# Which engine makes the lower parts in the first token block of a fused attention and two-layer gated network

## The chip, the cores and the metric

The kernel runs on one core of one Trainium2 chip. The metric is the device time of one execution in microseconds; lower is better.

## The reference, cut to what matters

Local attention (chunks of 32 queries, a window of 64 keys with 8 memory keys) gives x of 3072 tokens by 512. Two feed-forward layers follow, all in fp32:

```python
x = attention(q, k, v, mem_k, mem_v)            # 3072 x 512
gate = 1 / (1 + np.exp(-(x @ w_gate)))          # 512 -> 1536
x = (gate * (x @ w_val)) @ w_out                # 1536 -> 512
h = x @ w_in                                    # 512 -> 2048
out = (h * (1 / (1 + np.exp(-h)))) @ w_out2     # 2048 -> 512
```

## The kernel before, in words

**Products in three passes.** Every fp32 operand of a product is split in two: an upper part `hi`, which is the value cast to the matmul's type (ScalarE, `nc.scalar.copy`), and a lower part `lo = src - hi` (a subtraction with both inputs in SBUF). A product is then hi·hi + hi·lo + lo·hi, three matmuls of 128x512 each (helpers `split`, lines 77 to 85, `mm3`, lines 87 to 94, and `proj`, line 252). The upper part must be there before the lower part can be made.

**Stages.** The 3072 tokens are six blocks of 512 (`BLOCKS1`). Attention of the first block runs at the start; that of each later block is spread over the block before it. For each block, 12 iterations f do: pg = x·w_gate (12 matmuls), the sigmoid on ScalarE, pv = x·w_val (12 matmuls), the gate `sg = pv * sg` on VectorE (`gated`, L277), its split into g, and 12 matmuls y += g·w_out for the iteration before (`emit_out1`, L90 to L94). After the six blocks the second layer follows (L658 and L771). The order of each engine's queue is the order in which the program is written (`tc.manual_schedule()`).

**Weights of the first layer.** They arrive in a 64-bit layout and are turned into fp32 only once, during the first block, by 36 `Unit` objects: w_gate, w_val and w_out of each f. One unit is one load of 512 KB into a staging buffer `stg` (four of them), `rebias` on ScalarE (L107), `join`, three VectorE instructions of 128x512 (L115, L118, L122) that write the fp32 tile `t` (two buffers), and `part`, which splits t into the tile `u` that the matmuls read; a w_out unit is also written to DRAM (`keep`) for the later blocks. `Feed.step` (lines 145 to 156) is called three times in each iteration f of the first block and handles three units at once, in this order: `part` of unit k-2, `rebias` of unit k, `join` of unit k-1, then the load of a later unit.

```python
def part(self):
    self.u = self.slot(self.name)
    split(self.u[:, 0], self.u[:, 1], self.t, nc.gpsimd)
    if self.keep is not None:
        nc.sync.dma_start(out=self.keep, in_=self.u.bitcast(F32))
```

So in the first block GpSimd makes the lower parts of the 36 weight tiles and, by the table `GL`, those of the 12 gates g; two of the four lower parts of the first x (`split_x` with `NP = 2`) are GpSimd's as well. From the second block on VectorE makes the gates' lower parts itself, by L85.

**The places that matter.** pv of iteration f+1 is written into the PSUM bank that the gate of iteration f read, so TensorE waits there for VectorE's L277. In each iteration VectorE runs two joins before L277 and one behind it; the attention of the next block adds its reductions and products (L202, L203, L210 to L213, L236) in some iterations.

Of the kernel before, what the change touches and what calls it, by code (L numbers as in the profile page):

```python
# [8 lines left out]
F32 = mybir.dt.float32  # L9
# [3 lines left out]
ALU = mybir.AluOpType  # L13
# [16 lines left out]
BLOCKS1 = [512] * 6  # L30
NB2 = 3
NPAIR = NF2 // 2
GL = range(12)
NH = ()
NI = 7
LV = 1
# [11 lines left out]
def moe_kernel(ctx: ExitStack, tc: tile.TileContext, qh, kh, vh, wg, wv, wo, w2i, w2o, out):  # L48
    nc = tc.nc
# [29 lines left out]
    def split(hi, lo, src, lo_eng, hi_eng=nc.scalar):  # L79

        if hi_eng is nc.scalar:
            nc.scalar.copy(hi, src)  # L82
        else:
            hi_eng.tensor_copy(hi, src)
        lo_eng.tensor_tensor(out=lo, in0=src, in1=hi.bitcast(F32), op=ALU.subtract)  # L85
# [11 lines left out]
    class Unit:  # L97
# [26 lines left out]
                op0=ALU.logical_shift_left, op1=ALU.bitwise_or,  # L124
            )

        def part(self):
            self.u = self.slot(self.name)
            split(self.u[:, 0], self.u[:, 1], self.t, nc.gpsimd)
            if self.keep is not None:  # L130
                nc.sync.dma_start(out=self.keep, in_=self.u.bitcast(F32))

    class Feed:
# [10 lines left out]
        def step(self):  # L144
            k, u = self.n, self.units
            if k >= len(u) + 2:
                return
            self.load(k + 1)
            if 0 <= k - 2 < len(u):
                u[k - 2].part()  # L150
            if k < len(u):
                u[k].rebias()
            if 0 <= k - 1 < len(u):
                u[k - 1].join()
            self.load(k + self.AHEAD)
            self.n += 1

# [23 lines left out]
    def att_scores(t, ps_sc, e):  # L181
        sc = ps_sc(f"sc{t}")
        scv = sc.rearrange("p (c2 a k) -> p c2 a k", c2=2, a=4)
        qb, kt = q_t.pop(t), k_t.pop(t)
        for c2 in range(2):
            for a in range(4):
                for cp in range(2):
                    c = 2 * c2 + cp
                    nc.tensor.matmul(  # L189
                        scv[cp * 64 : cp * 64 + 64, c2, a],  # L190
                        qb[:, 4 * a + c].rearrange("p u q -> p (u q)"),
                        kt[:, a, c],
                        start=True,
                        stop=True,
                    )
        if t % TPB == 0:
            nc.vector.memset(scv[0:64, 0, :, NMEM : NMEM + LEFT], NEG)
        if t % TPB == TPB - 1:
            nc.vector.memset(scv[64:128, 1, :, WIN - RIGHT : WIN], NEG)
        s3 = sc.rearrange("p (g k) -> p g k", k=WIN)  # L200
        m = att.tile([P, 8, 1], F32, tag="m", name=f"m{t}", bufs=2)
        nc.vector.tensor_reduce(m, s3, axis=AX.X, op=ALU.max)  # L202
        nc.vector.tensor_tensor(out=e, in0=s3, in1=m.to_broadcast([P, 8, WIN]), op=ALU.subtract)  # L203
        nc.scalar.activation(out=e, in_=e, func=AF.Exp, scale=SCALE)
        e_t[t] = e

    def att_norm(t, eng=nc.vector):
        e = e_t[t]
        r = att.tile([P, 8, 1], F32, tag="r", name=f"r{t}", bufs=2)
        nc.vector.tensor_reduce(r, e, axis=AX.X, op=ALU.add)  # L210
        nc.vector.tensor_scalar_add(r, r, 1e-9)
        nc.vector.reciprocal(r, r)
        eng.tensor_tensor(out=e, in0=e, in1=r.to_broadcast([P, 8, WIN]), op=ALU.mult)  # L213

    def att_turn(t, ps_pt, at):
        e = e_t.pop(t).rearrange("p g k -> p (g k)")
        pt = ps_pt(f"pt{t}")
        for i in range(4):
            nc.tensor.transpose(pt[:, i * P : (i + 1) * P], e[:, i * P : (i + 1) * P], ident)
        nc.scalar.copy(at.rearrange("p a b q -> p (a b q)"), pt)  # L220
        at_t[t] = at

    def att_pv(t, ps_px, xt, off):
        at, vb = at_t.pop(t), v_t.pop(t)
        px = ps_px(f"px{t}")
        for c in range(4):
            for j in range(4):
                q0 = 64 * (c % 2) + 32 * (j % 2)
                nc.tensor.matmul(  # L229
                    px[32 * j : 32 * j + 32, c * P : (c + 1) * P],  # L230
                    at[:, c // 2, j // 2, q0 : q0 + 32],
                    vb[c * len(vb) // 4][:, :, c % (4 // len(vb)), j],
                    start=True,
                    stop=True,
                )
        nc.vector.transpose(  # L236
            out=xt[:, :, off : off + P].rearrange("p k (c q) -> p c k q", c=4),
            in_=px.rearrange("p (c k q) -> p c k q", c=4, k=4),
        )
# [33 lines left out]
        nc.scalar.activation(out=sg[:, :n], in_=psg[:, :n], func=AF.Sigmoid)  # L273
        return sg

    def gated(sg, psv, n, name, pool, bufs, lo_eng=nc.vector):
        nc.vector.tensor_tensor(out=sg[:, :n], in0=psv[:, :n], in1=sg[:, :n], op=ALU.mult)  # L277
        g = pool.tile([P, 2, 512], F32R, tag="g", name=f"g{name}", bufs=bufs)
        split(g[:, 0, :n], g[:, 1, :n], sg[:, :n], lo_eng)
        return g  # L280


    with tc.manual_schedule():
# [3 lines left out]
        p1 = p1_cm.__enter__()  # L287
# [53 lines left out]
        units = []  # L341
# [31 lines left out]
        def idle(n):  # L373
            for _ in range(n):
                nc.tensor.transpose(warm[:, :P], ident, ident)

        def prefetch(t):
            if t < NTILE:
                att_load_qk(t, qA, k_tile(t))

        def prefetch_v(t):
            if t < NTILE:
                att_load_v(t, vA)

        idle(22)
        for i in range(n0 + 2):
            if i < n0:
                att_scores(i, ps_y, es[i])
                idle(NI)
            if 0 <= i - 2 < n0:  # L390
                at = hold[0].tile([P, 512], F32, tag="sg", name=f"at{i - 2}", bufs=3)
                att_turn(i - 2, ps_a, at.rearrange("p (a b q) -> p a b q", a=2, b=2))
                idle(NI if i < 4 else 0)
            if 0 <= i - 1 < n0:
                att_norm(i - 1, nc.gpsimd if i - 1 in NQ else nc.vector)
            if 0 <= i - 3:
                att_pv(i - 3, ps_y, x32[0], (i - 3) * P)
                idle(NI if i < 4 else 0)
            if i == 1:
                prefetch(n0)  # L400
            if i == 4:
                prefetch_v(n0)
            if i == n0:
                units[0].rebias()
                units[0].join()
            if i == n0 + 1:
                units[0].part()
                units[1].rebias()
        att_pv(n0 - 1, ps_y, x32[0], (n0 - 1) * P)
        idle(NJ)  # L410
        x = split_x(x32.pop(0), BLOCKS1[0], "x0", NP, NH)
        units[1].join()
        units[2].rebias()
        feed1.n = 3
        feed1.step()
# [3 lines left out]
        for bi in range(NB1 - 1):  # L419
            n = BLOCKS1[bi + 1] // P  # L420
# [78 lines left out]
        g_t, wo_u, yacc = {}, {}, {}  # L499
# [296 lines left out]
                    done(A22, dp)  # L796


        pending = None
        prep = prepare2()  # L800
        xgen = None
        for bi, n in enumerate(BLOCKS1):
            last = bi == NB1 - 1
            if last:
                att_cm.__exit__(None, None, None)
                xr_cm = tc.tile_pool(name="xr", bufs=1, side="right")
                xr = xr_cm.__enter__()
                xgen = x_parts(0, *load_y0())
            for f in range(NF1):
                it = 3 * (bi * NF1 + f)  # L810

                def steps(i):
                    run_events(it + i)
                    if bi == 0:
                        feed1.step()
                    elif (it + i) % 3 != 0:
                        next(prep, None)
                    if last and (i == 2 and 1 < f < NF1):

                        if f >= 3:  # L820
                            next(xgen, None)

                psg = ps_m(f"pg{bi}_{f}")
                proj(psg, U1["g", f].u, x, n, late=None if bi else (0, 1) if f == 0 else (1, 0))
                sg = sigmoid(psg, n, f"{bi}_{f}")
                steps(0)
                psv = ps_m(f"pv{bi}_{f}")
                proj(psv, U1["v", f].u, x, n, late=None if bi else (1, 0))
                steps(1)
                if f == NF1 - 1 and not last:  # L830
                    x = split_x(x32.pop(bi + 1), BLOCKS1[bi + 1], f"x{bi + 1}")
                g_t[bi, f] = gated(sg, psv, n, f"{bi}_{f}", p1, 2, nc.gpsimd if bi == 0 and f in GL else nc.vector)
                if last and f == NF1 - 1:
                    for _ in range(NRING - 1):
                        next_granule()
                if pending is not None:
                    emit_out1(*pending)
                pending = (bi, f)
                steps(2)

        for _ in prep:
            pass
# [96 lines left out]
```

## Time and profile before

| what | value |
|---|---|
| median of 3 runs (lowest, highest) | 1166.29 us (1165.51, 1167.08) |
| the profiled execution's own time | 1165.85 us |
| its span, first to last instruction | 1164.1 us |
| TensorE matmul busy | 1138.2 us, 98% |
| VectorE busy | 695.6 us, 60%, 965 instructions |
| ScalarE busy | 487.4 us, 42% |
| GpSimd busy | 124.5 us, 11%, 94 instructions |
| first block: first pg to the second block's first pg | 27.70 to 160.54 us of the span |

Engines in the rows: PE is TensorE, DVE is VectorE, ACT is ScalarE, POOL is GpSimd, SP issues the DMAs. The shares are means over the whole span; the first block is about a ninth of it and has another balance than the rest, so it is read by windows of its own.

### The profile page before, as it was taken

The numbers are of one execution on the slowest core, as the hardware profiler recorded it, in microseconds if no ns is written. First come the engines' busy times: TensorE is split into PE (matmuls) and PEld (weight loads), VectorE is DVE, ScalarE is ACT, GpSimd is POOL, SyncE is SP. The second block draws the span as 40 slices with busy tenths as digits, with TensorE's granted clock in tenths as the row PEclk, the third lists the DMA queues.
The fourth block names the chain that finished last, engine by engine and source line by source line (L and its number), as shares of the span: only waits on it lengthen the run. The fifth ranks groups of instructions, "written<-read, shape, count | busy, mean of one in ns | idle before, by whom it ended". The sixth has DMA issues, their size and how long they took to land.

```text
span 1164.1 us, 16020 instructions
## 1 busy us (share of the span) xinstructions
PE 1138.2 (98%) x6319; PEld 927.7 (80%) x6319; DVE 695.6 (60%) x965; ACT 487.4 (42%) x708; POOL 124.5 (11%) x94
## 2 busy tenths in 40 slices
PE   8889999999999999999999999999999999999998
PEld 7667777888888888888887888888888888888887
DVE  7999965455555554554564534347944369634665
ACT  3555544334434433443343224445434454344442
POOL 2545530000000000000000001111001110011000
PEclk9999999999999999999999999999999999999999
DMA  9777767667656666766565356566655575655552
GB/s 314 244 238 246 242 218 238 208 206 227 224 194 212 219 227 194 242 213 203 199 205 211 120 188 199 190 239 237 228 199 192 205 282 215 227 193 203 208 204 86
DMA packets 79210, 248.51 MB, mean 213 GB/s; under 512 B 7584, under 2 KB 23968, under 8 KB 69920
## 3 DMA queue, kind: packets, MB, share of 16 engines
q1 hardware_dynamic: 79136, 247.49, 62.4%
q8 instruction: 50, 0.82, 0.3%
q14 instruction: 24, 0.20, 0.0%
HBM read 199.23 MB, written 48.23 MB: 213 GB/s over the span
## 4 chain that ended last, share of the span: by engine, by line
PE 83%; DVE 12%; DMA 3%; issue 1%; ACT 0%; SPq 0%; DVEq 0%; ACTq 0%
PE o L771 20%; PE c L658 20%; PE pv L263 13%; PE pg L263 13%; PE y L90 5%; PE y L92 5%; PE y L94 5%; PE sc L189 1%; PE px L229 1%; DVE t_wg L122 1%; DVE t_wo L122 1%; DVE t_wv L122 1%; DVE stg_wv L118 1%; DVE stg_wo L118 1%; DVE stg_wg L118 1%; DMA v<-in_vh_dram 1%
## 5 line engine op out<-in xcount | busy, mean ns | idle before, releaser
L658 PE MATMUL c<-xp,wr 128*128 128x512 f32 x1008 | 229.1, 389 | 0.0
L771 PE MATMUL o<-gf,wr 128*128 128x512 f32 x1008 | 229.0, 389 | 0.0
L263 PE MATMUL pv<-x,w 128*128 128x512 f32 x864 | 216.1, 400 | 13.0 <-DVE sg L277 11.4
L658 PEld LDWEIGHTS c<-xp,wr 128*128 128x128 f32 x1008 | 189.2, 188 | 39.3
L771 PEld LDWEIGHTS o<-gf,wr 128*128 128x128 f32 x1008 | 189.2, 188 | 39.3
L263 PE MATMUL pg<-x,w 128*128 128x512 f32 x864 | 210.6, 392 | 1.6 <-POOL x L85 0.9
L263 PEld LDWEIGHTS pv<-x,w 128*128 128x128 f32 x864 | 162.9, 191 | 51.9 <-issue 14.3
L263 PEld LDWEIGHTS pg<-x,w 128*128 128x128 f32 x864 | 160.4, 188 | 38.2 <-ACT x L82 1.5
L85 DVE TENSOR_TENSOR gf<-g,gf 128x1024 fp32r<-128x1024 f32 x84 | 103.8, 1239 | 49.9 <-ACT gf L82 49.6
L82 ACT CAST gf<-g 128x1024 fp32r<-128x1024 f32 x84 | 88.1, 1053 | 86.9 <-PE o L771 73.3
L678 POOL TENSOR_TENSOR s<-s,s 128x512 f32<-128x512 f32 x24 | 35.9, 1497 | 820.7 <-ACT s L677 820.7
L82 ACT CAST g<-sg 128x512 fp32r<-128x512 f32 x72 | 44.7, 621 | 156.8 <-DVE sg L277 156.8
L273 ACT ACTIVATE sg<-pg 128x512 f32<-128x512 f32 x72 | 42.9, 596 | 74.8 <-PE pg L263 61.7
L630 DVE TENSOR_TENSOR s<-c,s 128x512 f32<-128x512 f32 x48 | 33.2, 691 | 65.1 <-PE c L658 63.1
L90 PE MATMUL y<-g,wor 128*128 128x512 f32 x240 | 66.3, 397 | 0.6 <-DVE y L532 0.6
L85 DVE TENSOR_TENSOR g<-sg,g 128x512 fp32r<-128x512 f32 x60 | 41.5, 692 | 41.7 <-ACT g L82 41.7
L92 PE MATMUL y<-g,wor 128*128 128x512 f32 x240 | 64.3, 390 | 0.0
L94 PE MATMUL y<-g,wor 128*128 128x512 f32 x240 | 64.2, 389 | 0.0
L277 DVE TENSOR_TENSOR sg<-pv,sg 128x512 f32<-128x512 f32 x72 | 49.3, 684 | 21.3 <-PE pv L263 21.2
L633 DVE TENSOR_TENSOR g<-g,g 128x1024 f32<-128x1024 f32 x48 | 58.4, 1216 | 0.0
L636 ACT ACTIVATE g<-s 128x512 f32<-128x512 f32 x48 | 30.3, 632 | 54.1 <-DVE s L630 54.1
L92 PEld LDWEIGHTS y<-g,wor 128*128 128x128 f32 x240 | 45.1, 188 | 9.6
(120 smaller groups left out, 1127.3 us busy)
## 6 DMA issues: line engine op xcount, KB each, us to landing
wr<-w2o_d SPq DMA_DIRECT2D x42, 1024.0 KB, 4.8
wor<-wo_d SPq DMA_DIRECT2D x60, 512.0 KB, 4.7
wr<-w2i_d SPq DMA_DIRECT2D x24, 1024.0 KB, 5.0
wr<-w2i_d SPq DMA_DIRECT2D x24, 768.0 KB, 4.4
w2o_d<-coo SPq DMA_DIRECT2D x56, 256.0 KB, 2.8
w2i_d<-coi SPq DMA_DIRECT2D x24, 512.0 KB, 3.0
qA<-in_qh_dram SPq DMA_DIRECT2D x21, 512.0 KB, 4.9
k<-in_kh_dram SPq DMA_DIRECT2D x21, 512.0 KB, 5.5
```

Source lines behind the costliest of these rows:

```text
L82: nc.scalar.copy(hi, src)
L85: lo_eng.tensor_tensor(out=lo, in0=src, in1=hi.bitcast(F32), op=ALU.subtract)
L90: nc.tensor.matmul(o, w_hi, x_hi, start=first, stop=False)
L92: nc.tensor.matmul(o, w_hi, x_lo, start=False, stop=False)
L94: nc.tensor.matmul(o, w_lo, x_hi, start=False, stop=last)
L263: nc.tensor.matmul(o[:, :n], w[:, pw, kt * P : (kt + 1) * P], x[kt][:, px, :n], start=i == 0, stop=i == len(steps) - 1,)
L273: nc.scalar.activation(out=sg[:, :n], in_=psg[:, :n], func=AF.Sigmoid)
L277: nc.vector.tensor_tensor(out=sg[:, :n], in0=psv[:, :n], in1=sg[:, :n], op=ALU.mult)
L633: nc.vector.tensor_tensor(out=o, in0=a, in1=b_, op=ALU.subtract)
L658: nc.tensor.matmul(o, w[:, pw, i % 4, kt * P : (kt + 1) * P], X[i][:, px, kt], start=first and j == 0, stop=j == 5, skip_group_check=not f ...
L678: nc.gpsimd.tensor_tensor(out=s5, in0=s5, in1=s1, op=ALU.add)
L771: nc.tensor.matmul(c[at[i], dp], w[:, pw, pl, dp * P : (dp + 1) * P], f[:, px, pl], start=i in (A11, S1, S2) and pp == 0 and j == 0, stop= ...
```

## The change

GpSimd's 48 lower parts (36 weight tiles, 12 gates) go to VectorE. `part` is cut in two: `high` makes the upper part on ScalarE where `part` stood, and `rest` makes the lower part on VectorE, behind the join of the next unit; the DMA that keeps a w_out tile follows it. A gate's lower part is put in a list in the first block, and made after the third `Feed.step` of the iteration. The two lower parts of the first x stay on GpSimd.

```diff
-GL = range(12)
...
-        def part(self):
+        def high(self):
             self.u = self.slot(self.name)
-            split(self.u[:, 0], self.u[:, 1], self.t, nc.gpsimd)
+            nc.scalar.copy(self.u[:, 0], self.t)
+
+        def rest(self):
+            nc.vector.tensor_tensor(
+                out=self.u[:, 1], in0=self.t, in1=self.u[:, 0].bitcast(F32), op=ALU.subtract
+            )
             if self.keep is not None:
                 nc.sync.dma_start(out=self.keep, in_=self.u.bitcast(F32))
...
             self.load(k + 1)
+
             if 0 <= k - 2 < len(u):
-                u[k - 2].part()
+                u[k - 2].high()
             if k < len(u):
                 u[k].rebias()
             if 0 <= k - 1 < len(u):
                 u[k - 1].join()
+            if 0 <= k - 2 < len(u):
+                u[k - 2].rest()
             self.load(k + self.AHEAD)
...
-    def gated(sg, psv, n, name, pool, bufs, lo_eng=nc.vector):
+    def gated(sg, psv, n, name, pool, bufs, rest=None):
+
         nc.vector.tensor_tensor(out=sg[:, :n], in0=psv[:, :n], in1=sg[:, :n], op=ALU.mult)
         g = pool.tile([P, 2, 512], F32R, tag="g", name=f"g{name}", bufs=bufs)
-        split(g[:, 0, :n], g[:, 1, :n], sg[:, :n], lo_eng)
+        nc.scalar.copy(g[:, 0, :n], sg[:, :n])
+
+        def lo():
+            nc.vector.tensor_tensor(
+                out=g[:, 1, :n], in0=sg[:, :n], in1=g[:, 0, :n].bitcast(F32), op=ALU.subtract
+            )
+
+        lo() if rest is None else rest.append(lo)
         return g
...
             if i == n0 + 1:
-                units[0].part()
+                units[0].high()
                 units[1].rebias()
...
         units[1].join()
+        units[0].rest()
         units[2].rebias()
...
-        pending = None
+        pending, rests = None, []
...
-                g_t[bi, f] = gated(sg, psv, n, f"{bi}_{f}", p1, 2, nc.gpsimd if bi == 0 and f in GL else nc.vector)
+                g_t[bi, f] = gated(sg, psv, n, f"{bi}_{f}", p1, 2, None if bi else rests)
...
                 steps(2)
+                while rests:
+                    rests.pop()()
```

VectorE's queue at the start of the first block, before (x_0 and x_1 are the first tokens, t_wg_384 and t_wv_455 the fp32 tiles of the first gate and value weights, stg their staging buffers):

```order
L85 TENSOR_TENSOR x_0_443<-x_0_113,x_0_443 128x512
L85 TENSOR_TENSOR x_1_446<-x_0_113,x_1_446 128x512
L115 TENSOR_SCALAR stg_wv_138<-stg_wv_138 128x512
L118 SCALAR_TENSOR_TENSOR stg_wv_138<-stg_wv_138 128x512
L122 SCALAR_TENSOR_TENSOR t_wv_455<-stg_wv_138 128x512
L115 TENSOR_SCALAR stg_wg_140<-stg_wg_140 128x512
L118 SCALAR_TENSOR_TENSOR stg_wg_140<-stg_wg_140 128x512
L122 SCALAR_TENSOR_TENSOR t_wg_463<-stg_wg_140 128x512
```

and the same place now (the tile numbers and lines are shifted; L131 is `rest`, w_413 the weight tile that the first pg and pv read):

```order
L84 TENSOR_TENSOR x_0_442<-x_0_113,x_0_442 128x512
L84 TENSOR_TENSOR x_1_445<-x_0_113,x_1_445 128x512
L114 TENSOR_SCALAR stg_wv_138<-stg_wv_138 128x512
L117 SCALAR_TENSOR_TENSOR stg_wv_138<-stg_wv_138 128x512
L121 SCALAR_TENSOR_TENSOR t_wv_454<-stg_wv_138 128x512
L131 TENSOR_TENSOR w_413<-t_wg_384,w_413 128x512
L114 TENSOR_SCALAR stg_wg_140<-stg_wg_140 128x512
L117 SCALAR_TENSOR_TENSOR stg_wg_140<-stg_wg_140 128x512
L121 SCALAR_TENSOR_TENSOR t_wg_462<-stg_wg_140 128x512
L131 TENSOR_TENSOR w_413<-t_wv_454,w_413 128x512
L114 TENSOR_SCALAR stg_wv_142<-stg_wv_142 128x512
```

The first gate weight's lower part, which the first pg reads from its second matmul on, now stands behind the join of the first value weight.

VectorE's queue of one iteration without attention (f = 5), before:

```order
L277 TENSOR_TENSOR sg_4_858<-pv_4_870,sg_4_858 128x512
L115 TENSOR_SCALAR stg_wg_790<-stg_wg_790 128x512
L118 SCALAR_TENSOR_TENSOR stg_wg_790<-stg_wg_790 128x512
L122 SCALAR_TENSOR_TENSOR t_wg_918<-stg_wg_790 128x512
L115 TENSOR_SCALAR stg_wv_843<-stg_wv_843 128x512
L118 SCALAR_TENSOR_TENSOR stg_wv_843<-stg_wv_843 128x512
L122 SCALAR_TENSOR_TENSOR t_wv_950<-stg_wv_843 128x512
L115 TENSOR_SCALAR stg_wo_868<-stg_wo_868 128x512
L118 SCALAR_TENSOR_TENSOR stg_wo_868<-stg_wo_868 128x512
L122 SCALAR_TENSOR_TENSOR t_wo_972<-stg_wo_868 128x512
L277 TENSOR_TENSOR sg_5_937<-pv_5_956,sg_5_937 128x512
```

and its beginning now (L285 is the gate, L290 the gate's lower part):

```order
L285 TENSOR_TENSOR sg_4_858<-pv_4_870,sg_4_858 128x512
L114 TENSOR_SCALAR stg_wg_790<-stg_wg_790 128x512
L117 SCALAR_TENSOR_TENSOR stg_wg_790<-stg_wg_790 128x512
L121 SCALAR_TENSOR_TENSOR t_wg_915<-stg_wg_790 128x512
L131 TENSOR_TENSOR wo_912<-t_wo_890,wo_912 128x512
L290 TENSOR_TENSOR g_4_898<-sg_4_858,g_4_898 128x512
L114 TENSOR_SCALAR stg_wv_842<-stg_wv_842 128x512
L117 SCALAR_TENSOR_TENSOR stg_wv_842<-stg_wv_842 128x512
L121 SCALAR_TENSOR_TENSOR t_wv_949<-stg_wv_842 128x512
L131 TENSOR_TENSOR w_946<-t_wg_915,w_946 128x512
```

Four instructions were added between two gates: one `rest` behind each of the three joins, and the lower part of g behind the first of them. ScalarE's queue has the same 709 rows in the same order in both kernels, and SP's DMAs stand in the same order.

## Rows read from the trace of the kernel before

**Rows 1.** The page: busy us of each engine, share, instructions.

```profile
PE 1138.2 (98%) x6319; PEld 927.7 (80%) x6319; DVE 695.6 (60%) x965; ACT 487.4 (42%) x708; POOL 124.5 (11%) x94
```

**Rows 2.** Windows: length; busy PE, PEld, DVE, ACT, POOL; clock, DMA, GB/s.

```profile
41.90:154.90 113.00, 98.76 (x602) 76.09 (x600) 105.99 (x130) 60.92 (x96) 60.83 (x40) 0.97 0.69 233
163.10:276.10 113.00, 112.66 (x715) 90.91 (x714) 61.45 (x112) 45.09 (x69) 1.29 (x1) 1.00 0.68 231
```

**Rows 3.** Waits, 41.9 to 154.9 us: us in total, times, longest us.

```profile
PE pv L263 <- DVE sg L277: 9.7, 7, 2.2
```

**Rows 4.** Timeline of DVE in the first block: start us, us, engine line op.

```profile
58.58 0.69 DVE L118 SCALAR_TENSOR_TENSOR stg_wv<-stg_wv 128x512 int32<-128x512 int32 x1
59.38 1.60 DVE L122 SCALAR_TENSOR_TENSOR t_wv<-stg_wv 128x512 int32<-128x512 int32 x1
```

**Rows 5.** Timeline of POOL in the first block.

```profile
58.87 1.56 POOL L85 TENSOR_TENSOR w<-t_wg,w 128x512 fp32r<-128x512 f32 x1 [2.62 <-ACT w L82]
```

**Rows 6.** Windows of L122 alone, first and second block: DVE busy, clock, DMA.

```profile
41.90:154.90 113.00, 36.46 (x30) 0.97 0.69 233
180.00:300.00 120.00, 4.84 (x7) 1.00 0.68 224
```

**Rows 7.** Windows of L118 alone, first and second block: DVE busy, clock, DMA.

```profile
41.90:154.90 113.00, 28.12 (x30) 0.97 0.69 233
180.00:300.00 120.00, 4.86 (x7) 1.00 0.68 224
```

**Rows 8.** Windows of L115 alone, first and second block: DVE busy, clock, DMA.

```profile
41.90:154.90 113.00, 20.45 (x31) 0.97 0.69 233
180.00:300.00 120.00, 2.91 (x7) 1.00 0.68 224
```

**Rows 9.** Windows of L213 alone, first and second block: DVE busy, clock, DMA.

```profile
41.90:154.90 113.00, 6.03 (x4) 0.97 0.69 233
180.00:300.00 120.00, 3.46 (x5) 1.00 0.68 224
```

**Rows 10.** Windows of L277 alone, first block.

```profile
41.90:154.90 113.00, 6.80 (x10) 0.97 0.69 233
```

**Rows 11.** Timeline of DVE in the second block.

```profile
171.64 0.69 DVE L85 TENSOR_TENSOR g<-sg,g 128x512 fp32r<-128x512 f32 x1 [0.74 <-ACT g L82]
172.25 0.68 DVE L532 COPY y<-y 128x512 f32<-128x512 f32 x1
176.47 0.69 DVE L118 SCALAR_TENSOR_TENSOR stg_w2i<-stg_w2i 128x512 int32<-128x512 int32 x1
177.19 0.69 DVE L122 SCALAR_TENSOR_TENSOR fi<-stg_w2i 128x512 int32<-128x512 int32 x1
```

**Rows 12.** Timeline of PE, start and end of the first block.

```profile
27.70 2.98 PE L263 MATMUL pg<-x,w 128*128 128x512 f32 x11 [0.62 <-ACT x L82]
33.52 4.61 PE L263 MATMUL pv<-x,w 128*128 128x512 f32 x12 [1.43 <-ACT w L82]
152.26 1.08 PE L229 MATMUL px<-vA,at 128*32 128x128 f32 x32
157.82 1.07 PE L90 MATMUL y<-g,wo 128*128 128x512 f32 x4
160.54 2.99 PE L263 MATMUL pg<-x,w 128*128 128x512 f32 x12
```

**Rows 13.** Timeline of DVE: first join, and gates of iterations 0 and 10.

```profile
32.12 0.69 DVE L122 SCALAR_TENSOR_TENSOR t_wv<-stg_wv 128x512 int32<-128x512 int32 x1
41.22 0.68 DVE L277 TENSOR_TENSOR sg<-pv,sg 128x512 f32<-128x512 f32 x1
154.19 0.68 DVE L277 TENSOR_TENSOR sg<-pv,sg 128x512 f32<-128x512 f32 x1
```

**Rows 14.** Timeline of ACT behind the gate of iteration 2.

```profile
64.48 0.62 ACT L82 CAST g<-sg 128x512 fp32r<-128x512 f32 x1 [2.23 <-DVE sg L277]
65.01 0.62 ACT L82 CAST wo<-t_wo 128x512 fp32r<-128x512 f32 x1
```

## The prediction

> **What bounds the kernel now.** I read the page first: TensorE is busy for 98% of the span and VectorE for 60% [rows 1]. That is a mean, so the next view is the windows. In 113 us of the first block TensorE shows 98.8 us of work and VectorE 106.0 us; in 113 us of the second block TensorE shows 112.7 us and VectorE 61.5 us [rows 2]. The first block is VectorE's, the rest TensorE's. The waits say the same: in the first block TensorE stands 9.7 us in seven waits for L277, the gate, before it may start the next pv [rows 3]. So what VectorE saves between gates in this block, the block saves, down to TensorE's own work there. That work, at the rate of the second block (715 recorded matmuls in 112.7 us), is 602 / 715 x 112.7 = 94.9 us for 113.0 us elapsed.
>
> Next, what fills VectorE. In its timeline the same 128x512 instruction comes in two lengths: L118 at 58.58 us takes 0.69 us, L122 right behind it 1.60 us [rows 4]. GpSimd had started a lower part at 58.87 us [rows 5]. Line by line, against the second block, where GpSimd makes none: L122 takes 36.46 us for 30, against 4.84 us for 7 [rows 6]; L118 28.12 against 4.86 [rows 7]; L115 20.45 for 31, against 2.91 for 7 [rows 8]; L213 6.03 for 4, against 3.46 for 5 [rows 9]. L277, which reads one input from PSUM, stays at 0.68 us for each of 10 [rows 10]. GpSimd's work stretches VectorE's.
>
> **The change, part by part.** I take the stretch from the end of gate 0 (41.90 us) to the end of gate 10 (154.87 us), 112.97 us, then its two ends.
>
> *Removed: the stretching.* The excess over the second block's durations: L122 36.46 - 30 x 0.691 = 15.7; L118 28.12 - 30 x 0.694 = 7.3; L115 20.45 - 31 x 0.416 = 7.6; L213 6.03 - 4 x 0.692 = 3.3 [rows 6 to 9]. Together 33.8 us, beside 40 GpSimd instructions [rows 2], so 0.85 us each. Their own 60.8 us lie beside VectorE and count only through this.
>
> *Removed: a wait for GpSimd's semaphore.* L122 now waits for GpSimd to have read the buffer that it overwrites. It starts 0.80 us behind L118 in the first block [rows 4] and 0.72 us in the second, where there is no such wait [rows 11]. 30 x 0.08 = 2.4 us.
>
> *Added: 40 lower parts on VectorE.* In the second block the same instruction (L85) is 0.69 us long and the next starts 0.61 us behind it [rows 11]. 40 x 0.61 = 24.4 us, all on the path. The upper bound, 0.69 each, is 27.6.
>
> *Sum of the stretch:* -33.8 - 2.4 + 24.4 = -11.8 us, so 101.2 us, still above TensorE's 94.9. As a cross-check, three joins of 1.85 us (L115 0.42 [rows 8] and a gap of 0.10, then 0.72 and 0.61), four lower parts and a gate make 8.6 us for an iteration without attention. TensorE's loop there is pv (2.7 to 2.9), then y (2.72), which must wait until VectorE has made a join and two lower parts (3.1 us behind the gate), then pg (2.7 to 2.9): about 8.7 us. The two are nearly level, so I expect a few tenths of wait on either side, and a new wait of y for the gate's lower part.
>
> *The start.* The first pg reads the weight's lower part from its second matmul on. Before, GpSimd had it ready when pg began at 27.70 [rows 12]. Now it comes behind the join of the first value weight, whose last instruction starts at 32.12 [rows 13]; that join is still stretched, since GpSimd keeps two lower parts of x. It is ready at 32.12 + 0.61 + 0.69 = 33.4, and eleven matmuls follow. Warm, eleven took 2.98 us; the twelve at 33.52, behind a gap of 1.43 us, took 4.61 [rows 12]. Behind a gap of over 5 us I take the slow figure, about 4.3. Then the sigmoid and the next upper part (1.4 us), a lower part, a join, a lower part and the gate: gate 0 ends near 42.95 against 41.90 [rows 13], **+1.05**. With TensorE warm VectorE would set the pace and gate 0 end at about 41.5, -0.4.
>
> *The end.* Before, from gate 10 (end 154.87) to the second block's pg (160.54) it took 5.67 us. Now y(10) waits for its gate's lower part, 3.1 us behind the gate, and takes 2.72 (157.82 to 160.54, [rows 12]): 5.8. TensorE will also come late to that pv, since the last attention product (1.08 us, [rows 12]) then stands ahead of it with no slack left: up to +1.1. I take **+0.9**, bounds +0.1 and +1.2.
>
> *At nothing:* ScalarE does the same work in the same order. The upper part that a lower part waits for is made while VectorE joins: behind the gate ScalarE casts g and then the w_out tile, the two starting 0.53 us apart and each lasting 0.62 [rows 14], 1.2 us against a join's 1.85. The w_out store moves behind `rest` on SP's queue; loads queue behind it, as they do behind GpSimd's instruction now, and have three steps, some 8 us, to land. If one took longer, VectorE's next join would be late.
>
> *Sum:* -11.8 + 1.05 + 0.9 = -9.85. From the profiled execution's 1165.85 us that is **1156.0 us**. The median of the runs before is 0.4 us above that execution, so a median after it may read 0.4 more. The stages behind are TensorE's and shift as they are.
>
> **The rivals.**
>
> *TensorE becomes the bound (0.09).* pv took 4.61 us behind an idle gap instead of some 2.9 [rows 12]; the granted clock is 0.97 of full in the first block's window and 1.00 in the second's [rows 2], so part of the block already runs at 1.2 GHz instead of 2.4. With gaps of about 1 us left in each iteration, half of the ten pv's might be slow: 1.7 us each less the 0.6 to 0.7 us that TensorE has spare, 5 us in all. Time: 1161. Against it: the gaps get shorter than the present ones, up to 2.2 us [rows 3].
>
> *ScalarE's upper part comes late (0.05), slower.* Now VectorE itself waits for the upper part; before, only GpSimd did, and VectorE ran on. Everything behind `rest` on VectorE's queue, the gate too, would stand. Each of 30 `rest` may lose 0.39 us on average before the 11.8 us are gone; at 0.6 us each (ScalarE one cast further behind, [rows 14]) the stretch loses 18 and the time is 1165.85 - 9.85 + 18 = 1174. For it: ScalarE's order puts a gate's cast, which waits for VectorE, ahead of a weight's. Against it: the 1.2 against 1.85 us above.
>
> *VectorE was simply full (0.03), slower.* If the long forms are not GpSimd's doing but belong to this stage (the staging buffers are also written by DMA), 24.4 us come on top and nothing goes: 1165.85 + 24.4 + 2 = 1192. The Trainium skill bears on it: "Perfetto Trace Analysis", section "Optimizing Scalar/DVE Operations", says that work may be taken off a saturated VectorE, even to GpSimd, and adds that the two share a read port, so that this might not help. The first half of that speaks against this change. The rows speak for the second: L277 with its PSUM input is untouched and L213, which reads no staging buffer, is stretched [rows 9, 10].
>
> *No change (0.03):* gains and new stalls of some 10 us cancel, 1165.
>
> **How the numbers follow.** The forecast has 0.80, the partial gain 0.09, no change 0.03, the two slower cases 0.08. About 0.2%, 2.3 us, is what a measurement of this kernel can tell from none. Faster: 0.80 + 0.09 = 0.89; within: 0.03; slower: 0.08. The range's lower end takes the start at -0.4, the end at +0.1 and TensorE's waits at none: 1165.85 - 11.8 - 0.3 = 1153.8, less 0.7, the difference if the cross-check's steps are summed instead of the excesses: 1153. The upper end takes in the rival of TensorE, 1161, and 0.4 for the median: 1161.5. That leaves out some 0.15.
>
> **What would show it.** Right: GpSimd at 46 instructions and VectorE at 1013; L115, L118 and L122 back near 0.42, 0.69 and 0.69 us everywhere but in the first join; the stretch from gate 0 to gate 10 near 101 us; gate 0 about 1 us later, with a gap of over 5 us in the first pg; a new wait of y for the gate's lower part of a few us in sum; nothing changed behind the first block. Wrong: VectorE idle in front of `rest` for ScalarE (the second rival); slow matmuls in many iterations (the first); long forms left (the third); joins waiting for loads.

## The result, and the profile after

Four runs of the changed kernel have a median of 1155.3 us (1154.98 to 1156.31), four of the kernel before 1165.9 us (1165.5 to 1167.08): a ratio of 0.9905, 95% interval [0.9894, 0.9917]. The profiled executions are 10.9 us apart in span, 1164.1 and 1153.2 us.

The page of the changed kernel, the line that answers to [rows 1]:

```profile
PE 1133.1 (98%) x6319; PEld 926.5 (80%) x6319; DVE 685.9 (59%) x1013; ACT 487.8 (42%) x708; POOL 52.1 (5%) x46
```

VectorE has 48 instructions more and is busy 9.7 us less; GpSimd has 48 fewer. Where that happened is in the windows, the stretch from the end of gate 0 (44.15 us) to the end of gate 10 (144.94 us), and 113 us of the second block (columns as in [rows 2]):

```profile
44.15:144.94 100.79, 94.53 (x610) 74.52 (x609) 95.87 (x171) 60.43 (x96) 0.00 (x0) 1.00 0.77 261
152.30:265.30 113.00, 113.00 (x719) 91.83 (x718) 62.22 (x114) 45.27 (x69) 0.00 (x0) 1.00 0.68 229
```

The stretch took 112.97 us before and takes 100.79 us now. VectorE made 41 instructions more in it (the 40 lower parts, and a gate at the window's edge), in 10.1 us less of busy time. The windows of single lines show why, in this order L121, L117, L114 and L220, which were L122, L118, L115 and L213 [rows 6 to 9]:

```profile
44.15:144.94 100.79, 20.78 (x30) 1.00 0.77 261
```

```profile
44.15:144.94 100.79, 20.83 (x30) 1.00 0.77 261
```

```profile
44.15:144.94 100.79, 12.59 (x31) 1.00 0.77 261
```

```profile
44.15:144.94 100.79, 2.77 (x4) 1.00 0.77 261
```

36.46 became 20.78, 28.12 became 20.83, 20.45 became 12.59 and 6.03 became 2.77: 34.1 us of stretching are gone, against 33.8 in the prediction's ledger. The timeline of VectorE in this stretch shows one join with the lower part behind it, and the gate's:

```profile
64.88 0.69 DVE L117 SCALAR_TENSOR_TENSOR stg_wg<-stg_wg 128x512 int32<-128x512 int32 x1
65.61 0.69 DVE L121 SCALAR_TENSOR_TENSOR t_wg<-stg_wg 128x512 int32<-128x512 int32 x1
66.22 0.69 DVE L131 TENSOR_TENSOR wo<-t_wo,wo 128x512 fp32r<-128x512 f32 x1
66.82 0.68 DVE L290 TENSOR_TENSOR g<-sg,g 128x512 fp32r<-128x512 f32 x1
```

L121 starts 0.73 us behind L117 (0.80 before, [rows 4]), and each lower part takes 0.60 or 0.61 us of the queue. The waits in the same stretch:

```profile
PE pv L270 <- DVE sg L285: 5.2, 4, 2.1
PE y L91 <- DVE g L290: 1.0, 3, 0.4
```

TensorE's wait for the gate fell from 9.7 us in seven [rows 3] to 5.2 us in four, and the new wait of y for the gate's lower part is there, with 1.0 us. No wait of VectorE for ScalarE shows in the stretch.

The two ends. TensorE at the start of the first block and at its end (these answer to [rows 12]):

```profile
27.46 0.50 PE L270 MATMUL pg<-x,w 128*128 128x512 f32 x1 [0.51 <-ACT x L81]
33.20 4.67 PE L270 MATMUL pg<-x,w 128*128 128x512 f32 x11 [5.24 <-DVE w L131]
...
145.22 3.01 PE L270 MATMUL pv<-x,w 128*128 128x512 f32 x12
...
150.79 2.88 PE L270 MATMUL pg<-x,w 128*128 128x512 f32 x12
```

The first pg does one matmul and then stands 5.24 us for the weight's lower part. VectorE and ScalarE behind it, first the two lower parts around the wait and gate 0, then ScalarE's sigmoid:

```profile
40.39 0.69 DVE L131 TENSOR_TENSOR w<-t_wg,w 128x512 fp32r<-128x512 f32 x1 [2.91 <-ACT w L128]
...
43.47 0.68 DVE L285 TENSOR_TENSOR sg<-pv,sg 128x512 f32<-128x512 f32 x1
```

```profile
37.96 1.28 ACT L280 ACT_TABLE_LOAD   x1 [4.17 <-PE pg L270]
39.25 0.60 ACT L280 ACTIVATE sg<-pg 128x512 f32<-128x512 f32 x1
39.74 0.61 ACT L128 CAST w<-t_wg 128x512 fp32r<-128x512 f32 x1
```

Gate 0 ends 16.69 us behind the first pg, where it was 14.20 us. At the other end the second block's pg starts 5.85 us behind the end of gate 10, before 5.67.

### The profile page after: what moved, and what is told of

Same layout as the page of the kernel before. It is cut to its first block, busy times and chain, and to the rows that moved or that the text cites. A ratio compares the mean times of both kernels' runs of the same rounds, so it can differ in the third digit from the quotient of the medians.

```text
span 1153.2 us, 15956 instructions
## 1 busy us (share of the span) xinstructions
PE 1133.1 (98%) x6319; PEld 926.5 (80%) x6319; DVE 685.9 (59%) x1013; ACT 487.8 (42%) x708; POOL 52.1 (5%) x46
## 4 chain that ended last, share of the span: by engine, by line
PE 86%; DVE 9%; DMA 3%; issue 1%; ACT 1%; SPq 0%; DVEq 0%; ACTq 0%
PE o L787 20%; PE c L674 20%; PE pg L270 14%; PE pv L270 14%; PE y L89 5%; PE y L91 5%; PE y L93 5%; PE sc L196 2%; PE px L236 1%; DVE w L131 1%; DMA v<-in_vh_dram 1%; DVE stg_wv L117 1%; DVE sg L285 1%; PE pt L226 1%; DVE stg_wo L117 1%
## 5 line engine op out<-in xcount | busy, mean ns | idle before, releaser
L270 PE MATMUL pv<-x,w 128*128 128x512 f32 x864 | 211.2, 393 | 5.2 <-DVE sg L285 5.2
L270 PEld LDWEIGHTS pv<-x,w 128*128 128x128 f32 x864 | 160.0, 188 | 41.9 <-issue 8.6
L290 DVE TENSOR_TENSOR g<-sg,g 128x512 fp32r<-128x512 f32 x72 | 49.8, 691 | 42.6 <-ACT g L287 42.6
L285 DVE TENSOR_TENSOR sg<-pv,sg 128x512 f32<-128x512 f32 x72 | 49.4, 686 | 20.6 <-PE pv L270 20.5
```

The lines of the kernel that those rows point to most:

```text
L270: nc.tensor.matmul(o[:, :n], w[:, pw, kt * P : (kt + 1) * P], x[kt][:, px, :n], start=i == 0, stop=i == len(steps) - 1,)
L290: nc.vector.tensor_tensor(out=g[:, 1, :n], in0=sg[:, :n], in1=g[:, 0, :n].bitcast(F32), op=ALU.subtract)
```

## The experiments

Each is the changed kernel with one edit. "The stretch" is always from the end of gate 0 to the end of gate 10, 100.79 us in the changed kernel; gate 0 is given by its end. Theory: in the first block VectorE's queue sets the pace, and what GpSimd does there lengthens that queue by more than the same work costs on VectorE. Rival: VectorE was simply full, the long forms belong to the stage. Second rival: ScalarE's upper part, or TensorE, sets the pace.

### GpSimd makes the weights' lower parts once more

```diff
             nc.vector.tensor_tensor(
                 out=self.u[:, 1], in0=self.t, in1=self.u[:, 0].bitcast(F32), op=ALU.subtract
             )
+            nc.gpsimd.tensor_tensor(
+                out=self.u[:, 1], in0=self.t, in1=self.u[:, 0].bitcast(F32), op=ALU.subtract
+            )
```

> The changed kernel, in which GpSimd makes each of the 36 weights' lower parts a second time, right behind VectorE's, into the same place with the same values. Nothing is taken from VectorE. Theory (GpSimd's instructions stretch VectorE's by 0.85 us each, and VectorE's join waits 0.08 us more for GpSimd's semaphore): 30 x 0.93 = 28 us in the stretch from gate 0 to gate 10 and 1 or 2 us at the start: about 1184 us, the means of L114, L117, L121 and of the lower parts well above 0.42, 0.69, 0.69, 0.69. Rival (the long forms belong to the stage, not to GpSimd): only the semaphore's 2.4 us, about 1158 us, all forms short.

Measured: 1183.06 us (one run), the stretch 122.54 us, 21.75 us more; gate 0 at 47.42 us. VectorE executes the same instructions as in the changed kernel. Its timeline, with GpSimd's instruction between:

```profile
63.37 0.69 DVE L293 TENSOR_TENSOR g<-sg,g 128x512 fp32r<-128x512 f32 x1
...
63.53 1.68 POOL L134 TENSOR_TENSOR wo<-t_wo,wo 128x512 fp32r<-128x512 f32 x1 [3.62 <-DVE wo L131]
...
63.97 1.53 DVE L114 TENSOR_SCALAR stg_wv<-stg_wv 128x512 int32<-128x512 int32 x1
...
71.03 0.68 DVE L288 TENSOR_TENSOR sg<-pv,sg 128x512 f32<-128x512 f32 x1
...
71.19 1.28 POOL L134 TENSOR_TENSOR w<-t_wv,w 128x512 fp32r<-128x512 f32 x1 [2.03 <-DVE w L131]
...
71.63 1.12 DVE L114 TENSOR_SCALAR stg_wg<-stg_wg 128x512 int32<-128x512 int32 x1
```

The long forms are back, on the instruction that starts while GpSimd's runs: L114 takes 1.53 us there and ends 0.29 us behind GpSimd's end. The one that VectorE has under way when GpSimd starts keeps its length, L293 with its two SBUF inputs too. The timeline of the kernel before shows the same: inside 38 of the 40 GpSimd instructions of the stretch a long form starts; the 29 of L122, L118 and L213 end 0.54 to 0.56 us behind GpSimd's end (60.98 against 60.43 us in [rows 4, 5]), the nine of L115 0.28 to 0.30 us behind it. So VectorE is held until GpSimd is done, and the price is what is left of GpSimd's instruction by then. VectorE's busy time in the stretch rises from 95.87 to 115.17 us, 0.64 us for each of 30, and the semaphore adds the rest. The rival that VectorE was simply full gives 1158 us and falls. The size was overstated: 0.64 rather than 0.85 us. Here GpSimd starts each time right behind VectorE's lower part; in one of three places the gate is under way by then, which is not lengthened, and the L114 behind it meets less of GpSimd's instruction: 1.12 us instead of 1.53.

### VectorE makes the weights' lower parts once more

```diff
             nc.vector.tensor_tensor(
                 out=self.u[:, 1], in0=self.t, in1=self.u[:, 0].bitcast(F32), op=ALU.subtract
             )
+            nc.vector.tensor_tensor(
+                out=self.u[:, 1], in0=self.t, in1=self.u[:, 0].bitcast(F32), op=ALU.subtract
+            )
```

> The changed kernel, in which VectorE makes each of the 36 weights' lower parts twice, the same instruction once more. Theory (VectorE's queue sets the stretch, 0.61 us for each further lower part): 30 x 0.61 = 18.3 us between gate 0 and gate 10 and some 1.8 us at the start: about 1175.4 us. Beside the repeat by GpSimd this gives the price of the same work on either engine: 0.61 against 0.93. Rival (TensorE nearly sets the pace by now, so VectorE has spare time): clearly less than 18 us, under 1168 us.

Measured: 1180.25 us (one run), the stretch 122.53 us, 21.74 more; gate 0 at 46.62 us. The theory's sign and place hold, TensorE hides none of it. The size is 0.72 us each, not 0.61: the repeat writes what the instruction ahead of it wrote, so it starts only behind that one's end.

```profile
62.27 0.68 DVE L131 TENSOR_TENSOR wo<-t_wo,wo 128x512 fp32r<-128x512 f32 x1
62.99 0.69 DVE L134 TENSOR_TENSOR wo<-t_wo,wo 128x512 fp32r<-128x512 f32 x1
63.59 0.69 DVE L293 TENSOR_TENSOR g<-sg,g 128x512 fp32r<-128x512 f32 x1
```

The second starts 0.72 us behind the first, the next, independent one 0.60 behind that. So the two repeats cost the stretch the same 21.7 us, and I may not set 0.61 against 0.93 as the expectation did. What the pair does show is that an instruction which VectorE does not execute costs its queue as much as a dependent one that it does.

### The gates' lower parts on GpSimd again

```diff
-    def gated(sg, psv, n, name, pool, bufs, rest=None):
+    def gated(sg, psv, n, name, pool, bufs, rest=None, lo_eng=nc.vector):
...
         def lo():
-            nc.vector.tensor_tensor(
+            lo_eng.tensor_tensor(
...
-                g_t[bi, f] = gated(sg, psv, n, f"{bi}_{f}", p1, 2, None if bi else rests)
+                g_t[bi, f] = gated(sg, psv, n, f"{bi}_{f}", p1, 2, None, nc.vector if bi else nc.gpsimd)
```

> The changed kernel, with the 12 gates' lower parts of the first block back on GpSimd and the 36 weights' still on VectorE. Theory (a lower part costs VectorE 0.61 us when it makes it and 0.85 us when GpSimd makes it beside): 10 of them lie between gate 0 and gate 10, so the stretch grows by 10 x 0.24 = 2.4 us, from 100.8 to 103.2, and the time is 1157.7 us; some ten or more of VectorE's instructions show the long form again. Rival (VectorE was simply full and its long forms are not GpSimd's doing): VectorE loses 10 x 0.61 us of work and the time falls to 1149 us, no long forms.

Measured: 1159.02 us (1158.81 to 1159.78), ratio to the kernel before 0.9939 [0.9925, 0.9954]. The stretch takes 103.63 us, 2.84 more (expected 2.4). This undoes a quarter of the change, and VectorE, relieved of ten instructions, is the slower for it. In the windows of L121 alone the ten GpSimd instructions show:

```profile
45.12:148.75 103.63, 26.64 (x30) 1.00 0.75 254
```

5.86 us more than the 20.78 of the changed kernel. With L117 (21.73, 0.90 more), L114 (12.96, 0.37 more) and L220 (4.45, 1.68 more) that is 8.8 us for ten, 0.88 each, against 0.60 that VectorE saves: 2.8 us net. The long ones are ten, one for each of GpSimd's: six of L121, two of L220, one each of L117 and L114. The rival's 1149 us is far off. The median is 3.7 us above the changed kernel's, 2.4 were expected: in the profiled executions, 4.8 us apart, 1.0 us more lies ahead of the end of gate 0 and 1.2 us behind the second block's first pg.

### GpSimd only writes

```diff
             nc.vector.tensor_tensor(
                 out=self.u[:, 1], in0=self.t, in1=self.u[:, 0].bitcast(F32), op=ALU.subtract
             )
+            nc.gpsimd.memset(self.t, 0.0)
```

> The changed kernel, in which GpSimd clears each fp32 weight tile t (128x512) when both parts have been made from it, 36 instructions that write SBUF and read nothing; the tile is dead by then. The join that writes the tile next waits for GpSimd's semaphore. Theory A (any GpSimd instruction in SBUF stretches VectorE's): some 0.3 us or more for each of the 30 in the stretch, beside the semaphore's 0.08: 10 to 25 us more, 1165 to 1180 us. Theory B (only GpSimd's reading collides with VectorE's second input): the semaphore's 30 x 0.08 = 2.4 us alone, about 1157.7 us, with L117, L121 and the lower parts at 0.69 us; L114, which has one input and is the fast form, may be touched. The Trainium skill, page "SBUF - State Buffer", section "Who interferes with whom", says that a VectorE instruction with two SBUF inputs collides with a GpSimd instruction that reads SBUF and not with one that only writes it, which is theory B.

Measured: 1160.04 us (one run), the stretch 103.23 us, 2.44 more. That is the 30 x 0.08 us of the semaphore. Few of VectorE's instructions meet the clearing in a way that tells: L291, the gate's lower part, is under way when it starts, and would keep its length beside a subtraction too; L121 never overlaps it. The seven that tell are the L117 behind the clearing of a gate weight's tile:

```profile
62.91 0.42 DVE L114 TENSOR_SCALAR stg_wo<-stg_wo 128x512 int32<-128x512 int32 x1
63.11 0.69 POOL L134 MEMSET t_wg<- 128x512 f32 x1 [2.61 <-DVE w L131]
63.43 0.69 DVE L117 SCALAR_TENSOR_TENSOR stg_wo<-stg_wo 128x512 int32<-128x512 int32 x1
64.23 0.69 DVE L121 SCALAR_TENSOR_TENSOR t_wo<-stg_wo 128x512 int32<-128x512 int32 x1
```

and the same place where GpSimd subtracts, from the run in which it repeats the lower parts:

```profile
67.78 1.39 POOL L134 TENSOR_TENSOR w<-t_wg,w 128x512 fp32r<-128x512 f32 x1 [2.57 <-DVE w L131]
68.14 1.57 DVE L117 SCALAR_TENSOR_TENSOR stg_wo<-stg_wo 128x512 int32<-128x512 int32 x1
```

Held to the clearing's end as it was to the subtraction's, L117 would take some 0.9 us, an estimate from the 0.37 us that are left of the clearing and the 0.55 us behind its end; it takes 0.69 or 0.70 in all seven. L121 starts 0.80 us behind L117 here, where the changed kernel has 0.73: this is the semaphore alone, with nothing stretched. So theory B holds in these seven, for an instruction with two SBUF inputs, as the Trainium skill's page "SBUF — State Buffer" ("Who interferes with whom") has it. The clearing is also shorter than the subtraction (0.5 to 0.7 us against 1.3 to 1.7), so that GpSimd's reading is what makes the difference is argued from one run, and only for a short write. Nothing shows for L114: where it starts beside a clearing, at most 0.14 us of that is left. In these seven places the clearing takes 0.68 to 0.70 us, in the others 0.52 or 0.53: there GpSimd is the one that loses time, whether to L114 or to L117 the run does not tell. The remaining 2.3 us of the run's 4.7 lie outside the stretch; gate 0 alone is 1.3 us later.

### The lower part asked for at once

```diff
             if 0 <= k - 2 < len(u):
                 u[k - 2].high()
+                u[k - 2].rest()
             if k < len(u):
                 u[k].rebias()
             if 0 <= k - 1 < len(u):
                 u[k - 1].join()
-            if 0 <= k - 2 < len(u):
-                u[k - 2].rest()
```

> The changed kernel, with the lower part asked of VectorE right behind the order to ScalarE for the upper part, ahead of the next unit's join instead of behind it. The instructions are the same ones. Theory (the place behind the join is what hides ScalarE): in each iteration VectorE waits about 0.2, 0.75 and 1.2 us at its three weight parts (join to upper part, the last of them behind the gate's cast too), 2.1 us, so 10 iterations cost 21 us: about 1176 us, with a wait of VectorE's lower parts for ScalarE of some 20 us in sum. Rival (TensorE's own work or the loads set the pace, VectorE has slack): under 4 us more, below 1160 us.

Measured: 1176.84 us (one run), the stretch 119.85 us, 19.1 more (expected 21). The waits of VectorE between 46 and 167 us, a window around the stretch (46.62 to 166.47):

```profile
DVE wo L131 <- ACT wo L128: 9.8, 8, 1.7
DVE w L131 <- ACT w L128: 8.4, 10, 1.2
```

18.2 us in 18 waits, with the same instructions: this is the second rival's mechanism, and the place behind the join is what keeps it out of the changed kernel. Moved without that, the work would have cost more than it brought: 1176.84 us is slower than the kernel before.

### The first lower part earlier

```diff
-        x = split_x(x32.pop(0), BLOCKS1[0], "x0", NP, NH)
-        units[1].join()
         units[0].rest()
+        x = split_x(x32.pop(0), BLOCKS1[0], "x0", NP, NH)
+        units[1].join()
```

> The changed kernel, with the first gate weight's lower part made by VectorE ahead of the split of the first x instead of behind the join of the first value weight. Theory (the start's loss is this one instruction's place): the gap of 5.24 us in the first pg goes, gate 0 ends near 40.5 us of the span instead of 44.15, the stretch from gate 0 to gate 10 keeps its 100.8 us, and the time is 1155.3 - 3.6 = 1151.7 us. Rival (the start is set by the loads and the attention in front): the time stays at 1155.3 us, and gate 0 moves by less than 0.5 us.

Measured: 1152.26 us (1151.73 to 1152.67), ratio to the kernel before 0.988 [0.9863, 0.9896]. Gate 0 ends at 40.70 us, 3.45 earlier, and the stretch keeps 101.24 us. VectorE's timeline before the first pg and TensorE's:

```profile
26.76 0.65 DVE L131 TENSOR_TENSOR w<-t_wg,w 128x512 fp32r<-128x512 f32 x1
27.57 1.29 DVE L84 TENSOR_TENSOR x<-x,x 128x512 fp32r<-128x512 f32 x2 [0.16 <-ACT x L81]
28.78 1.52 DVE L114 TENSOR_SCALAR stg_wv<-stg_wv 128x512 int32<-128x512 int32 x1
```

```profile
27.59 2.99 PE L270 MATMUL pg<-x,w 128*128 128x512 f32 x11 [0.50 <-ACT x L81]
```

The lower part fits where VectorE was idle for the upper parts of x, and the gap of 5.24 us is gone. Since the difference to the changed kernel is small, both were measured once more, side by side:

> The changed kernel once more, on the same chip and in the same call as the kernel with the first gate weight's lower part moved forward, so that the two can be set side by side. Expected: 1155.3 us, as before.

> The changed kernel with the first gate weight's lower part ahead of the split of the first x, beside the changed kernel itself. Theory: 3 us under it, 1152.3 us, with intervals that do not touch. Rival (the 3 us between the first runs of the two were the chip's): within 1 us of it.

The changed kernel: 1156.31 us (1154.58 to 1157.12), ratio 0.9912 [0.9897, 0.9926]. With the first lower part earlier: 1152.65 us (1151.85 to 1152.87), ratio 0.9883 [0.9866, 0.9899]. The intervals overlap at their ends, so the expectation that they don't is missed; the runs themselves do not overlap, and the medians are 3.7 us apart, 3.0 in the first pair.

### No GpSimd in the first block at all

```diff
-NP = 2
+NP = 0
```

on top of the edit before.

> The changed kernel with the first gate weight's lower part ahead of the split of the first x, and with all four lower parts of that x on VectorE, so that GpSimd does nothing in the first block. Theory: the first join, which took 1.50, 1.64 and 0.69 us beside GpSimd's two, falls by 2.0 us, and two more lower parts cost VectorE 1.2 us; gate 0 ends 0.8 us before that of the kernel with the first part alone, 1150.9 us. Rival (TensorE's first pg and pv, not VectorE, set gate 0 by then): no difference to the kernel with the first part alone, within 0.3 us.

Measured: 1152.31 us (1150.36 to 1152.82), ratio 0.9877 [0.9859, 0.9895]. The same as with the first part alone; the rival's number holds. The first join is short again (L114 0.42, L117 0.69 us), but gate 0 ends 12.91 us behind the first pg instead of 13.11. Not TensorE holds it, as the rival had it: VectorE waits for the next load, which it did not reach so early before.

```profile
37.73 0.43 DVE L114 TENSOR_SCALAR stg_wo<-stg_wo 128x512 int32<-128x512 int32 x1 [0.31 <-DMA stg_wo<-in_wo_dram]
38.50 0.69 DVE L117 SCALAR_TENSOR_TENSOR stg_wo<-stg_wo 128x512 int32<-128x512 int32 x1 [0.34 <-ACT stg_wo L106]
```

These two waits take 0.65 of the 0.8 us that the edit was worth.

## Why the prediction was right, and which terms were off

The forecast was 1156.0 us, the median 1155.3. The steps one by one, in the profiled executions:

- **What bounds the block.** VectorE from gate to gate: shown by VectorE's repeat, which adds its full price to the stretch, and by the stretch, 100.79 us against 95.87 us of VectorE's busy time and the gaps between its instructions, with TensorE at 94.53.
- **The stretch.** Forecast -11.8 us (-12.5 by the cross-check), measured -12.18. The removed stretching was 34.1 (forecast 33.8); the semaphore 0.07 to 0.08 us each, shown alone by the run in which GpSimd only writes; the added parts 0.60 to 0.61 us.
- **The start: the term that was too small.** Forecast +1.05, measured +2.49 (gate 0 against the first pg; +2.04 in the changed kernel's second trace). The late lower part, the gap and the slow matmuls behind it came as written, with 4.67 us for eleven instead of about 4.3. What was left out is the load of the sigmoid's table on ScalarE: it stands behind the same wait for pg, so its 1.28 us came on top of the sigmoid before the next upper part could be made, and VectorE stood 2.91 us. Before, the load stood in that place too (34.09 us), but VectorE did not wait for ScalarE there. Moving that one lower part takes the loss away, and a little more.
- **The end: too large.** Forecast +0.9, measured +0.18. TensorE was not late at the pv that waits for gate 10: it starts 0.28 us behind the gate's end.
- **Behind the block: forecast nothing, measured -1.15 us**, so the sign "nothing changed behind the first block" failed (span -10.9, of which -9.75 at the second block's first pg: -0.24 before the first pg, +2.49, -12.18 and +0.18). A hint is in SP's queue. There the last w_out store waited for GpSimd's lower part, and the first load of the second layer's weights, issued 1.15 us behind that pg before, is now issued 0.57 us ahead of it. VectorE's wait for it falls from 5.10 to 2.60 us, and TensorE's wait of 0.22 us for VectorE, in front of the transposes of the second block's third iteration, is gone. VectorE's first join and those transposes, before and now:

```profile
168.16 0.43 DVE L115 TENSOR_SCALAR stg_w2i<-stg_w2i 128x512 int32<-128x512 int32 x1 [5.10 <-DMA stg_w2i<-in_w2i_dram]
184.56 0.63 PE L219 MATMUL pt<-ident,e 128*128 128x128 f32 x4 [0.22 <-DVE e L213]
```

```profile
156.45 0.43 DVE L114 TENSOR_SCALAR stg_w2i<-stg_w2i 128x512 int32<-128x512 int32 x1 [2.60 <-DMA stg_w2i<-in_w2i_dram]
173.86 0.60 PE L226 MATMUL pt<-ident,e 128*128 128x128 f32 x4
```

From that pg to these transposes it took 24.02 us before and takes 23.07 now, in the changed kernel's second trace too: 0.95 of the 1.15 us. With the gates' lower parts back on GpSimd the load is issued 0.57 us behind the pg again, VectorE waits 5.56 us for it and the transposes come after 23.78 us. There the w_out store waits for VectorE and not for GpSimd, so it is the late load that goes with the loss, whatever made it late. This was read off the traces and not tried by itself. The other 0.2 us is no more than two executions of the changed kernel differ: the second trace has -0.77 instead of -1.15 behind the block.
- **The rivals.** ScalarE late: possible, and seen, with the lower part asked for at once; kept out by the order. TensorE slow: the granted clock in the stretch is 1.00 (0.97 before); with the same work and more idle time, in the run with the parts asked for at once, it was 0.91. A lower clock need not cost time here: in VectorE's repeat it was 0.93, and the stretch grew by just VectorE's 30 x 0.72 us. VectorE simply full, and with it the rule to unload a full VectorE: refuted from both sides, by GpSimd's repeat and by the gates' return to GpSimd.

The errors are +1.4 us at the start, -0.7 at the end, -0.4 in the stretch, -1.15 behind the block and -0.24 ahead of the first pg; together they make -1.05. The stretch, which is the mechanism, was right; that the total is closer than the start alone is luck.

## What to carry to other kernels

A helper engine is free only if it doesn't lengthen the instructions of the engine that it relieves: compare the same instruction's duration in a stage with the helper and in one without, multiply, and set that against what the busy engine would pay itself. What such an instruction costs depends on how much of it is left when the busy engine starts its next one. When work moves onto an engine with an in-order queue, put each piece behind something as long as what it waits for, and look apart at the first piece, which has nothing ahead of it to hide behind. When a wait is lengthened, everything queued behind it on the waiting engine counts, a table load too.

## What the runs showed of the hardware that was not expected

- A GpSimd subtraction holds up a VectorE instruction with two SBUF inputs that starts beside it until GpSimd is done, and leaves the one under way alone: the held one ended 0.54 to 0.56 us behind GpSimd's end. L115, with one SBUF input, is held too (0.28 to 0.30 us); the reduction over e, with one, is not: in GpSimd's repeat it starts beside three subtractions and takes 0.68 us.
- So GpSimd's price to VectorE is not one number: 0.85 us for a 128x512 subtraction before, 0.88 for the gates' alone, 0.64 where it starts right behind VectorE's own lower part.
- GpSimd instructions that only write, 0.5 to 0.7 us long, cost VectorE nothing but the semaphore, 0.08 us for each join that waits for one more engine.
- Two VectorE instructions of 128x512 that write the same place start 0.72 us apart, two independent ones 0.60.
